# A windowed attention block feeding a gated feed-forward layer, on one core: V loaded by SyncE in fp32, masks of batch 0 added by matmul, one PSUM tile for both transposes, and a reordered opening with dummy matmuls

## The chip, the core and the metric

One core of one Trainium2 chip. The metric is device time in microseconds (us) of one execution. Before the change it was 290.46 us (median of 3 runs, 289.55 to 290.52). The profile's span, first to last instruction, is a little shorter than the timed run: 286.8 us in a run of 288.47 us. Differences are therefore taken between runs or between spans, never across.

Engine names are those of the profile: PE = TensorE, DVE = VectorE, ACT = ScalarE, POOL = GpSimd, SP = SyncE.

## The reference

```python
scores = (q @ k.T) / 8                     # q, k, v: 4 batches, 8 heads, 768 positions, 64 wide
keep   = (key < 4) | (0 <= query - key < 128)      # 4 sink keys and a window of 128
a      = softmax(where(keep, scores, -1e9))
x      = (a @ v), heads side by side       # 3072 tokens x 512
out    = (relu(x @ w_gate) * (x @ w_val)) @ w_out  # 512 -> 1536 -> 512, fp32 in and out
```

## The kernel before

Work is cut into units. A unit is a pair of heads of one batch: for batch 0 its first query half ("L", 4 units) or its second ("M", 4 units), for batches 1 to 3 all queries ("F", 12 units). Each unit's K, Q and V are loaded, cast to bf16, K and Q transposed on PE, then scores, exponentials, sums and V products follow in segments of 124 keys; the four sink keys are written into four spare rows of later segments. Beside this, PE works through the feed-forward layer in chunks: four gate matmuls, four value matmuls, then output matmuls. The four L units stand in an opening before the first chunk; all others are dealt out between chunks by a plan.

The parts that the change touches:

```python
def load_v(self, eng):                     # M and F: casting DMA from POOL straight into the bf16 tile
    dst = self.staging("v") if self.kind == "L" else self.vn
    for h in range(2):
        eng.dma_start(out=dst[:, j0:j0 + nj, h, 0:64], in_=...)

def T(self, pool, shape, tag, qcopy=nc.scalar.copy):
    ps = ptile("tk")                       # a PSUM tile for K ...
    for t in range(kn_): nc.tensor.transpose(ps[...], kn[s][...], ident[...])
    nc.scalar.copy(kT[s][...], ps[...])
    pq = ptile("tq")                       # ... and another for Q
    for t in range(qn_): nc.tensor.transpose(pq[...], qn[s][...], ident[...])
    qcopy(qT[s][...], pq[...])
    # [cut]

def S(self, gi):                           # scores of one group of segments
    # [cut: matmuls into ps, start=True, stop=True]
    nc.scalar.activation(x, ps[:, :, 0:c], Act.Exp, bias=0.0, scale=scale)
    nc.vector.tensor_tensor(x, x, bc(msk[:, m0:m0 + c], 2), op=Alu.mult)

def norm(u, part):
    ps = u.V(part)                         # sums and V products, in a two-bank attention tile
    nc.vector.transpose(r[:, 0, 0:w], ps[:, 1, 0:w])
    nc.vector.reciprocal(rc[...], r[...])
    nc.vector.transpose(r[:, 1, 0:w], ...)
    nc.vector.tensor_tensor(xTs[u.b][...], ps[:, 0, ...], r[:, 1, ...], op=Alu.mult)

# stages beside the feed-forward: after the last scores of a unit
u.S(gi)
if gi == len(u.groups) - 1:
    u.sinkv(nc.vector)                     # sink rows of V, on DVE
    if at(x + 2) is not None and x > NP:
        at(x + 2).load_v(nc.gpsimd)
```

PSUM holds three one-bank tiles for gate and value results ("gv"), one for outputs and two two-bank tiles ("at") that scores, transposes and normalisations share in turn.

The softmax here doesn't subtract the row's maximum and nothing guards it: scores larger than these inputs give would overflow.

Of the kernel before, what the change touches and what calls it, by code (L numbers as in the profile page):

```python
# [37 lines left out]
MW = 1417  # L38


@with_exitstack
def kernel(
# [33 lines left out]
    stg = [const.tile([128, 1536], F32, name=f"stg{i}") for i in range(3)]  # L76
    kn = [const.tile([128, 6, 2, 64], BF16, name=f"kn{i}") for i in range(2)]
    vn = [const.tile([128, 7, 2, 64], BF16, name=f"vn{i}") for i in range(3)]
    qn = [const.tile([128, 6, 2, 64], BF16, name=f"qn{i}") for i in range(2)]
# [11 lines left out]
    msk = const.tile([128, MW], BF16, name="msk")  # L91

# [4 lines left out]
    class Unit:  # L97


        def __init__(self, i, b, p, kind):  # L100
            self.i, self.b, self.p, self.kind, self.s, self.s3 = i, b, p, kind, i % 2, i % 3
            g = GEO[kind]
            self.q0, self.n, self.js, self.sink, self.groups, self.parts = (
                g[x] for x in ("q0", "n", "js", "sink", "groups", "parts"))
            (self.qr, self.qp, self.qn), (self.kr, self.kp, self.kn) = g["q"], g["k"]
            self.j5 = [j for j in self.js if j < 6]
            self.vn = vn[self.s3]
            self.where = {}
            for gi, segs in enumerate(self.groups):
                c = 0  # L110
                for j, qa, w in segs:
                    self.where[j] = (gi, c, qa)
                    c += w

        def staging(self, x):

            t, nk, nq = stg[self.s3], self.kn * 128, self.qn * 128
            if x == "v":
                return t[:, nk + nq:nk + nq + 128 * len(self.js)].rearrange("p (j h d) -> p j h d", h=2, d=64)
            return (t[:, 0:nk] if x == "k" else t[:, nk:nk + nq]).rearrange("p (h c) -> p h c", h=2)  # L120
# [9 lines left out]
        def load_v(self, eng):  # L130

            b, p = self.b, self.p
            dst = self.staging("v") if self.kind == "L" else self.vn
            j0, nj = self.j5[0], len(self.j5)
            for h in range(2):
                src = v[b, 2 * p + h]
                eng.dma_start(out=dst[:, j0:j0 + nj, h, 0:64],  # L137
                              in_=bass.AP(src.tensor, src.offset + 124 * j0 * D, [[D, 128], [124 * D, nj], [1, D]]))
            if 6 in self.js:
                eng.dma_start(out=dst[0:24, 6, :, 0:64],  # L140
                              in_=v[b, 2 * p:2 * p + 2, 744:768, :].rearrange("h s d -> s h d"))

        def cast(self, what, eng):

            s = self.s
            cp = eng.tensor_copy
            if what in "kq":
                dst, pp, nn = (kn[s], self.kp, self.kn) if what == "k" else (qn[s], self.qp, self.qn)
                cp(dst[0:pp, 0:nn, :, :],  # L149
                   self.staging(what)[0:pp, :, :].rearrange("p h (n d) -> p n h d", d=64))  # L150
                return
            cp(self.vn[:, 0:len(self.js), :, 0:64], self.staging("v"))
            cp(vsink[:, self.p, :, :], self.vn[0:4, 0, :, 0:64])
            self.sinkv(eng)
# [7 lines left out]
        def T(self, pool, shape, tag, qcopy=nc.scalar.copy):  # L162
# [3 lines left out]

            def ptile(name):
                t = pool.tile(shape, BF16, name=name, tag=tag)
                return t[:, 0, :] if len(shape) == 3 else t[:]
            ps = ptile("tk")  # L170
            for t in range(kn_):
                nc.tensor.transpose(ps[:, t * kp:(t + 1) * kp],  # L172
                                    kn[s][0:kp, t, :, :].rearrange("p h d -> p (h d)"), ident[0:kp, 0:kp])
# [3 lines left out]
            pq = ptile("tq")  # L177
            for t in range(qn_):
                nc.tensor.transpose(pq[:, t * qp:(t + 1) * qp],  # L179
                                    qn[s][0:qp, t, :, :].rearrange("p h d -> p (h d)"), ident[0:qp, 0:qp])  # L180
# [25 lines left out]
        def S(self, gi):  # L206
            s = self.s
            ps = ps_at.tile([128, 2, 512], F32, name="sps", tag="at")
            c = 0
            for j, qa, w in self.groups[gi]:  # L210
                for h in range(2):
                    r = slice(64 * h, 64 * h + 64)
                    nc.tensor.matmul(out=ps[:, h, c:c + w], lhsT=self.kw(j, r), rhs=qT[s][r, qa:qa + w],  # L213
                                     start=True, stop=True)
# [3 lines left out]
            m0 = MCOL[self.kind][gi]  # L218
            nc.vector.tensor_tensor(x, x, bc(msk[:, m0:m0 + c], 2), op=Alu.mult)  # L219

        def V(self, part):
# [3 lines left out]
            ps = ps_at.tile([128, 2, 512], F32, name="ops", tag="at")  # L225
            for what in range(2):
                for i, (j, qa, w) in enumerate(segs):
                    gi, c, qg = self.where[j]
                    c += qa - qg
                    for h in range(2):  # L230
                        nc.tensor.matmul(out=ps[64 * h:64 * h + 64, 1 - what, qa - q0:qa - q0 + w],  # L231
# [16 lines left out]
    def setup_pool():  # L248
        make_identity(nc, ident)
        t0, a = msk[:, 0:255], msk[:, 503:754]  # L250
        for x, w, d in ((t0, 255, 0), (a, 251, 4)):
            nc.gpsimd.memset(x, 1.0)
            nc.gpsimd.affine_select(out=x, in_=x, compare_op=Alu.is_ge, fill=0.0, base=d,
                                    pattern=[[1, w]], channel_multiplier=-1)
            nc.gpsimd.affine_select(out=x, in_=x, compare_op=Alu.is_ge, fill=0.0, base=127 - d,
# [7 lines left out]
    def setup_m0():  # L263

        ms(msk[0:4, 0:128], 1.0)
        ms(msk[0:4, 128:255], 0.0)
        cp(msk[:, 255:503], msk[:, 503:751])
        ms(msk[0:4, 255:503], 1.0)
        ms(msk[0:4, 503:627], 0.0)

    def setup_m1():

        band, sk = (lambda a, b: msk[:, 503 + a:503 + b]), (lambda n: msk[:, 255:255 + n])
        cp(msk[:, 754:1002], sk(248))
        cp(msk[:, 1002:1253], band(0, 251))
        cp(msk[:, 1253:1397], sk(144))
        cp(msk[:, 1397:1417], band(0, 20))
# [4 lines left out]
    def norm(u, part):  # L282
# [4 lines left out]
        ps = u.V(part)  # L287
        r = rpool.tile([128, 2, 416], F32, name="R")
        rc = dpool.tile([128, 13], F32, name="rc")
        nc.vector.transpose(r[:, 0, 0:w], ps[:, 1, 0:w])  # L290
# [4 lines left out]
        nc.vector.tensor_tensor(xTs[u.b][:, u.p, lo:hi], ps[:, 0, lo - c0:hi - c0], r[:, 1, lo - c0:hi - c0], op=Alu.mult)  # L295
# [36 lines left out]
    with tc.manual_schedule():  # L332
# [12 lines left out]
        for p in range(3):  # L345
            U[p].load_kq(nc.sync)
            U[p].load_v(nc.scalar if p == 0 else nc.sync)
        setup_pool()
        nc.scalar.activation(ee[0][:, 0, 0, 0:128], ident[:], Act.Exp, bias=0.0, scale=1.0)
        setup_slot(0)  # L350
        for s in range(3):
            nc.vector.memset(vn[s][:, 6, :, :], 0.0)
        nc.vector.memset(ones[:], 1.0)
# [3 lines left out]
        def next_load(x):  # L357

            w = at(x + 3)
            if w is not None:  # L360
                w.load_kq(nc.sync)
                if w.kind == "L":
                    w.load_v(nc.sync)

        casts(U[0], "kqv")
        next_load(0)
        setup_m0()
        U[0].T(*GV)
        setup_slot(1)
        casts(U[1], "kqv")  # L370
        next_load(1)
        U[1].T(*GV)
        for p in range(NP):
            for gi in range(2):
                U[p].S(gi)
            if p + 2 < NP:
                casts(U[p + 2], "kq" if p else "kqv")
                U[p + 2].T(*GV)
                if p == 0:
                    next_load(2)  # L380
            if p < 2:
                load_w(p)
            if p >= 1:
                norm(U[p - 1], 0)
                if p == 1:
                    casts(U[3], "v")
                    next_load(3)
                else:
                    U[p + 2].load_v(nc.gpsimd)
            if p >= 2:  # L390
                casts(U[p + 2], "kq")
                next_load(p + 2)
                load_w(p)
        norm(U[NP - 1], 0)
        U[6].load_v(nc.gpsimd)
        setup_m1()


        stages = []
        def unit_stages(x):  # L400
            u, prev, nxt = U[x], at(x - 1), at(x + 1)

            def s(gi):
                def f():
# [3 lines left out]
                    if gi == len(u.groups) - 1:  # L408
                        u.sinkv(nc.vector)
                        if at(x + 2) is not None and x > NP:  # L410
                            at(x + 2).load_v(nc.gpsimd)
# [6 lines left out]
            def t():  # L418
                if nxt is not None:
                    nxt.T(*AT)  # L420
                if at(x + 2) is not None:
                    casts(at(x + 2), "kq")
                    next_load(x + 2)
# [10 lines left out]
        blocks = [(0, 0, 376), (0, 376, 392)]  # L434
        for b in range(1, B):
            blocks += [(b, 0, S // 2), (b, S // 2, S // 2)]
# [4 lines left out]
        PLAN = ((0, 0), (3, 0), (12, 19), (23, 43), (47, 67), (71, 89), (72, 90))  # L441
# [6 lines left out]
        for bi, (b, c0, n) in enumerate(blocks):  # L448
            if c0 == 0 and b:
                hTs[b] = hpool.tile([128, FM, S], BF16, name="hT", tag="hT")  # L450
            for m in range(FM):
                while si < min(total, want(bi * FM + m)):
                    stages[si]()
                    si += 1
                chunk(b, c0, n, m)
                left = FM - m
                for _ in range((len(f2) + left - 1) // left):
                    f2.popleft()()
            done = c0 + n
            for t in range(6):  # L460
                lo, hi = t * 128, (t + 1) * 128
                if hi <= done and hi > c0:
# [39 lines left out]
```

## Time and profile before

The page of this kernel and a cut of its span into four stretches stand in the prediction below. PE's idle time in them (length less busy time) is 14.2 us in the opening, 7.3 and 6.4 us in the two halves of batch 0, and 3.7 us in the rest.

How the DMA engines are used is in the queue lines of the page (packets, MB, share of 16 engines over the span):

```profile
q0 software_dynamic: 30128, 7.71, 27.3%
q1 hardware_dynamic: 16224, 19.96, 21.8%
```

The software queue (POOL) moves a quarter of the bytes in two thirds of the packets and takes more of the engines' time.

### The profile page before, as it was taken

The numbers are of one execution on the slowest core, as the hardware profiler recorded it, in microseconds if no ns is written. First come the engines' busy times: TensorE is split into PE (matmuls) and PEld (weight loads), VectorE is DVE, ScalarE is ACT, GpSimd is POOL, SyncE is SP. The second block draws the span as 40 slices with busy tenths as digits, with TensorE's granted clock in tenths as the row PEclk, the third lists the DMA queues.
The fourth block names the chain that finished last, engine by engine and source line by source line (L and its number), as shares of the span: only waits on it lengthen the run. The fifth ranks groups of instructions, "written<-read, shape, count | busy, mean of one in ns | idle before, by whom it ended". The sixth has DMA issues, their size and how long they took to land.

```text
span 286.8 us, 5306 instructions
## 1 busy us (share of the span) xinstructions
PE 255.2 (89%) x2056; PEld 144.4 (50%) x2056; DVE 164.2 (57%) x347; ACT 130.3 (45%) x218; POOL 80.7 (28%) x123
## 2 busy tenths in 40 slices
PE   1567897867879989999999999999999999999994
PEld 0243454534545555555555556555555555555541
DVE  2379479966869885655666655745565642232210
ACT  3650375635655555353645545364553323333321
POOL 7959646842523532320405032300000000000000
PEclk9999999999999999999999999999999999999999
DMA  8999999993429454261914150331010000111112
GB/s 187 275 231 229 245 249 260 226 203 110 31 72 215 29 68 145 17 161 39 171 40 32 40 65 7 46 52 39 0 39 37 13 26 37 39 38 38 39 43 103
DMA packets 47178, 28.21 MB, mean 98 GB/s; under 512 B 28720, under 2 KB 44080, under 8 KB 47152
## 3 DMA queue, kind: packets, MB, share of 16 engines
q0 software_dynamic: 30128, 7.71, 27.3%
q1 hardware_dynamic: 16224, 19.96, 21.8%
q8 instruction: 16, 0.26, 0.4%
q10 hardware_dynamic: 800, 0.20, 0.3%
q14 instruction: 10, 0.08, 0.1%
HBM read 29.26 MB, written 6.29 MB: 124 GB/s over the span
## 4 chain that ended last, share of the span: by engine, by line
PE 80%; DVE 8%; ACT 4%; DMA 3%; issue 2%; POOL 1%; SPq 0%; ACTq 0%; POOLq 0%
PE gp L305 23%; PE op L324 22%; PE vp L311 21%; PE ops L231 7%; PE sps L213 4%; ACT ee L217 3%; DMA stg<-in_q_dram 3%; PE tk L172 2%; DVE R L293 2%; DVE xT L295 2%; DVE R L290 2%; PE tq L179 2%; DVE ee L219 1%; ACT kT L175 1%; DVE kTs L199 1%
## 5 line engine op out<-in xcount | busy, mean ns | idle before, releaser
L305 PE MATMUL gp<-xT,wg 128*128 128x384 bf16 (+2 forms) x384 | 80.4, 331 | 3.5 <-DVE xT L295 3.5
L308 ACT ACTIVATE gs<-gp 128x384 f32<-128x384 f32 (+2 forms) x96 | 47.3, 493 | 78.5 <-PE gp L305 77.1
L311 PE MATMUL vp<-xT,wv 128*128 128x384 bf16 (+2 forms) x384 | 79.1, 329 | 0.0
L313 DVE TENSOR_TENSOR hT<-gs,vp 128x384 bf16<-128x384 f32 (+2 forms) x96 | 52.5, 547 | 42.5 <-PE vp L311 40.0
L324 PE MATMUL op<-wo,hT 128*128 128x512 bf16 x288 | 75.9, 379 | 0.0
L217 ACT ACTIVATE ee<-sps 128x1006 bf16<-128x1006 f32 (+4 forms) x52 | 46.6, 906 | 32.0 <-PE sps L213 32.0
L219 DVE TENSOR_TENSOR ee<-ee,msk 128x1006 bf16<-128x1006 bf16 (+4 forms) x52 | 33.7, 655 | 34.1 <-ACT ee L217 34.0
L311 PEld LDWEIGHTS <-wv 128*128 128x128 bf16 x384 | 37.9, 99 | 29.2 <-issue 4.9
L137 POOL DMA_DIRECT2D vn<-in_v_dram x32 | 26.1, 818 | 80.5 <-PE ops L231 79.6
L305 PEld LDWEIGHTS <-wg 128*128 128x128 bf16 x384 | 32.8, 98 | 26.4 <-issue 5.6
L324 PEld LDWEIGHTS <-hT 128*128 128x128 bf16 x288 | 28.2, 98 | 25.1
L290 DVE STREAM_TRANSPOSE R<-ops 128x384 f32<-128x384 f32 (+1 forms) x32 | 18.7, 586 | 14.6 <-PE ops L231 14.6
L328 ACT COPY ot<-op 128x512 f32<-128x512 f32 x24 | 14.1, 586 | 22.3 <-PE op L324 22.3
L149 POOL CAST kn<-stg 128x768 bf16<-128x768 f32 (+2 forms) x20 | 15.9, 796 | 21.2 <-issue 20.9
L175 ACT COPY kT<-tk 128x768 bf16<-128x768 bf16 (+2 forms) x20 | 14.0, 700 | 16.9 <-PE tk L172 15.0
L231 PE MATMUL ops<-ee,ones 128*64 128x144 bf16 (+9 forms) x280 | 17.6, 250 | 2.6 <-ACT ee L217 1.7
L231 PEld LDWEIGHTS <-ones 128*64 128x64 bf16 x280 | 13.0, 112 | 13.7 <-issue 9.3
L213 PE MATMUL sps<-qT,kT 64*128 64x251 bf16 (+3 forms) x136 | 15.6, 257 | 4.4 <-ACT ee L217 2.6
L231 PE MATMUL ops<-ee,vn 128*64 128x144 bf16 (+9 forms) x280 | 17.2, 246 | 2.5 <-DVE vn L160 2.5
L293 DVE STREAM_TRANSPOSE R<-rc 128x384 f32<-128x384 f32 (+1 forms) x32 | 18.6, 583 | 1.1
L172 PE MATMUL tk<-ident,kn 128*128 128x128 bf16 (+2 forms) x108 | 9.7, 226 | 9.9 <-POOL kn L149 9.1
L295 DVE TENSOR_TENSOR xT<-ops,R 128x384 bf16<-128x384 f32 (+2 forms) x32 | 17.8, 558 | 1.1
(47 smaller groups left out, 151.5 us busy)
## 6 DMA issues: line engine op xcount, KB each, us to landing
out_dram<-ot SPq DMA_DIRECT2D x24, 256.0 KB, 2.0
stg<-in_k_dram SPq DMA_DIRECT2D x12, 384.0 KB, 4.6
stg<-in_q_dram SPq DMA_DIRECT2D x12, 384.0 KB, 5.3
vn<-in_v_dram POOLq DMA_DIRECT2D x24, 96.0 KB, 3.6
wg<-in_moe_w_gate_dram POOLq DMA_DIRECT2D x4, 384.0 KB, 7.8
wv<-in_moe_w_val_dram POOLq DMA_DIRECT2D x4, 384.0 KB, 8.9
wo<-in_moe_w_out_dram POOLq DMA_DIRECT2D x3, 512.0 KB, 7.7
stg<-in_k_dram SPq DMA_DIRECT2D x4, 280.0 KB, 5.2
```

Source lines behind the costliest of these rows:

```text
L137: eng.dma_start(out=dst[:, j0:j0 + nj, h, 0:64], in_=bass.AP(src.tensor, src.offset + 124 * j0 * D, [[D, 128], [124 * D, nj], [1, D]]))
L213: nc.tensor.matmul(out=ps[:, h, c:c + w], lhsT=self.kw(j, r), rhs=qT[s][r, qa:qa + w], start=True, stop=True)
L217: nc.scalar.activation(x, ps[:, :, 0:c], Act.Exp, bias=0.0, scale=scale)
L219: nc.vector.tensor_tensor(x, x, bc(msk[:, m0:m0 + c], 2), op=Alu.mult)
L231: nc.tensor.matmul(out=ps[64 * h:64 * h + 64, 1 - what, qa - q0:qa - q0 + w], lhsT=self.vn[:, j, h, :] if what else ones[:], rhs=ee[s][:, ...
L290: nc.vector.transpose(r[:, 0, 0:w], ps[:, 1, 0:w])
L293: nc.vector.transpose(r[:, 1, 0:w], bass.AP(a.tensor, a.offset, [a.ap[0], [1, nb], [0, 32]]))
L305: nc.tensor.matmul(out=gp[:, 0:n], lhsT=wg[:, ko, m * 128:(m + 1) * 128], rhs=x[:, ko, c0:c0 + n], start=ko == 0, stop=ko == KO - 1)
L308: nc.scalar.activation(gs[:, 0:n], gp[:, 0:n], Act.Relu, bias=0.0, scale=1.0)
L311: nc.tensor.matmul(out=vp[:, 0:n], lhsT=wv[:, ko, m * 128:(m + 1) * 128], rhs=x[:, ko, c0:c0 + n], start=ko == 0, stop=ko == KO - 1)
L313: nc.vector.tensor_tensor(hT[:, m, c0:c0 + n], gs[:, 0:n], vp[:, 0:n], op=Alu.mult)
L324: nc.tensor.matmul(out=op, lhsT=hTs[b][:, m, t * 128:(t + 1) * 128], rhs=wo[:, m, :], start=m == 0, stop=m == FM - 1)
```

## The change

Its intent: take work off DVE and waits off PE in the opening and beside batch 0, and get the transfers in earlier. Cut to its core:

```diff
-    stg = [const.tile([128, 1536], F32, name=f"stg{i}") for i in range(3)]
+    stg = [const.tile([128, 2432], F32, name=f"stg{i}") for i in range(4)]
     # kn, qn: 2 -> 3 buffers, vn: 3 -> 4
 def load_v:
-            dst = self.staging("v") if self.kind == "L" else self.vn
+            dst, o = self.staging("v"), self.js[0]          # fp32, by SP, all units
 def cast("v"):                                              # on POOL
+            cp(self.vn[:, j0:j0 + nj, :, :], self.staging("v")[:, 0:nj, :, :])
+            if 6 in self.js:
+                cp(self.vn[0:24, 6, :, :], self.staging("v")[0:24, nj, :, :])
             self.sinkv(eng)                                 # now for every kind, on POOL
 def T:
-            ps = ptile("tk")    # ... copy ...    pq = ptile("tq")
+            both = pool.tile(shape, BF16, name="tkq", tag=tag)    # all transposes, then both copies
 def S:
+            if biased:                                      # kinds L and M
+                for h in range(2):
+                    nc.tensor.matmul(out=ps[:, h, 0:n], lhsT=ident[:], rhs=bias[:, m0:m0 + n], start=True, stop=False,
+                                     skip_group_check=True)
-                                     start=True, stop=True)
+                                     start=not biased, stop=True, skip_group_check=True)
-            nc.vector.tensor_tensor(x, x, bc(msk[:, m0:m0 + c], 2), op=Alu.mult)
+            if not biased:
+                nc.vector.tensor_tensor(x, x, bc(msk[:, m0:m0 + c], 2), op=Alu.mult)
 def V (in the opening):
+                ps = [pool.tile([128, 512], F32, name=x, tag="gv")[:] for x in ("sums", "ops")][::-1]
 opening:
+        warm(16) ... warm(6) ... 4 x warm(8) ... warm(16)   # dummy matmuls of 128 columns
         # K and Q casts of units 2 and 3 come before V casts, loads of units 0 to 3 first of all
 stages:
+                if x >= 5:
+                    held(x + 8 - 5)                         # load K, Q, V of the unit three ahead
+                if at(x + 3) is not None:
+                    casts(at(x + 3), "kqv")
-        PLAN = ((0, 0), (3, 0), (12, 19), (23, 43), ...
+        PLAN = ((0, 0), (2, 0), (10, 19), (23, 43), ...
# [cut: the bias tile with 0 and -1e30, the mask made from it, order of loads]
```

## The prediction

> **What bounds the kernel now.** I read the page first (busy shares, the 40 slices), then one table of stretches, then the TensorE and VectorE timelines of the first 30 us, then TensorE's waits. The page:
>
> ```profile
> PE 255.2 (89%) x2056; PEld 144.4 (50%) x2056; DVE 164.2 (57%) x347; ACT 130.3 (45%) x218; POOL 80.7 (28%) x123
> PE   1567897867879989999999999999999999999994
> DMA  8999999993429454261914150331010000111112
> ```
>
> A slice is 7.2 us. From the fifteenth on PE is full; before it, it is not. So I cut the span where the work changes: start of the first gate/value matmuls, start of batch 0's second half, start of batch 1. Columns: length, busy time of each engine, clock, DMA share.
>
> ```profile
> 0.00:27.50 27.50, 13.27 (x104) 7.67 (x105) 15.24 (x44) 11.27 (x22) 22.28 (x47) 1.00 1.15 232
> 27.50:62.30 34.80, 27.55 (x268) 16.95 (x268) 26.28 (x55) 18.72 (x31) 22.33 (x32) 1.00 1.33 244
> 62.30:104.60 42.30, 35.87 (x370) 21.41 (x370) 32.72 (x67) 23.18 (x34) 16.08 (x21) 1.00 0.51 84
> 104.60:286.80 182.20, 178.55 (x1318) 98.41 (x1316) 89.99 (x183) 77.11 (x132) 20.00 (x26) 1.00 0.24 54
> ```
>
> The last 182 us are TensorE-bound (3.65 us idle, nearly all after the last matmul). No chunk of that part changes, so whatever the change is worth must come from the first 104.6 us: 14.2 us of idle PE in the opening, 7.3 + 6.4 us in batch 0. In the opening the chain of waits runs through VectorE, which normalises four head pairs and multiplies masks:
>
> ```profile
> 20.82 0.55 DVE xT L295
> 21.37 2.14 DVE ee L219 x2
> 23.51 0.50 DVE R L290
> ...
> 26.86 0.56 DVE xT L295
> 27.46 0.47 PE gp L305
> ```
>
> Look at the 2.14 us of masks in the middle. Then TensorE itself is slow when it starts:
>
> ```profile
> 27.73 1.46 PE L311 MATMUL vp<-xT,wv 128*128 128x376 bf16 x4
> 28.98 1.46 PE L305 MATMUL gp<-xT,wg 128*128 128x376 bf16 x4
> 30.24 1.16 PE L311 MATMUL vp<-xT,wv 128*128 128x376 bf16 x4
> 31.23 0.80 PE L305 MATMUL gp<-xT,wg 128*128 128x376 bf16 x4
> ```
>
> Starts are 1.25, 1.26, 0.99 us apart, and from 31.23 on 0.64 us, though the granted-clock column says 1.00 throughout. TensorE's waits between 28 and 105 us:
>
> ```profile
> PE ops L231 <- DVE vn L160: 2.5, 2, 1.2
> PE tq L179 <- ACT kT L175: 2.3, 3, 0.9
> PE ops L231 <- ACT ee L217: 1.7, 2, 1.1
> PE gp L305 <- DVE xT L295: 1.7, 1, 1.7
> PE sps L213 <- DVE kTs L199: 1.3, 2, 1.0
> PE tq L179 <- ACT ee L217: 0.7, 1, 0.7
> ```
>
> None names a DMA, although the DMA engines are full for 65 us.
>
> **What the Trainium skill says.** "TensorE: Matmul & The Clock Gate", section Part 1: an idle array runs at 1.2 GHz and goes to 2.4 GHz after about 3.4 us of sustained activity. The trace agrees: 376 columns took 313 ns (1.25/4), then 160. The same page, Part 3: matmuls in different row groups run concurrently. Here the two heads' 64-row score matmuls do (at 120.90 a 251-column pair, and the next pair starts 0.12 us later); a bias matmul uses all 128 rows and cannot. "DMA: Bandwidth & Descriptors", section SWDGE vs HWDGE vs iDMA: a cast inside a DMA is possible only from GpSimd, and there software writes the descriptors. Before does that for V: each pair of V issues holds Pool about 1.6 us. "SBUF — State Buffer", section Who interferes with whom: a VectorE instruction with two SBUF inputs and a GpSimd instruction that reads SBUF exclude each other. The trace fits: the two mask multiplies at 21.29 lasted 2.22 us beside casts, against means of 745 + 469 ns, and the query cast there 1.09 against a 0.74 mean.
>
> **The change part by part.** The fp32 loads and the block-transpose normalisation exist already; new are these.
>
> (a) Masks of batch 0 become bias matmuls. VectorE loses four multiplies of about 0.75 + 0.47 us before the first chunk (4.7 us with the contention) and eight of about 0.6 us in the second stretch. TensorE gains, per second-half unit, 2 x (399 + 415) columns: 1628 / 2.4 GHz = 0.68 us, x 4 = 2.7 us, on the bound engine. The first-half ones fall into idle time.
>
> (b) The opening is reordered: K/Q casts of units 2 and 3 come ahead on Pool, normalisation uses other PSUM banks, 70 dummy matmuls keep PE busy. I walked the engines with durations of the trace. Pool: setup to 3.9 (as now); unit 0 to 6.5, unit 1 to 8.9, K/Q of unit 2 to 9.95, first weight issues to 11.6, K/Q of unit 3 to 12.8 (now 14.1). PE: transposes of unit 1 to 8.0; at the cold rate its list is then solid (scores 1.6 with bias, 8 dummies 0.85, transposes 0.85, normalisation sums 1.25 each), so it should turn warm at about 12.5. From there ScalarE leads: transposed copies 1.2 us and exponentials 1.01 + 0.39 per unit: unit 3's copies end at 15.3, unit 2's exponentials at 16.7, unit 3's at 18.5. Sums of unit 3: 18.5 to 19.2. VectorE needs 2.05 us per normalisation (0.58 + 0.23 + 0.58 + 0.55, and gaps): 14.1 to 16.1, 16.1 to 18.2, 18.2 to 20.2, 20.2 to 22.25. First chunk's fourth matmul at 22.3 instead of 27.46: -5.2 us.
>
> (c) Warm start: the three slow groups above lose 0.61 + 0.62 + 0.35: -1.6 us.
>
> (d) Waits in batch 0. K and Q transposes share one PSUM tile, so the Q transposes no longer wait for a copy: 2.3 + 0.7 = -3.0 us. The sink rows of V are written on Pool a unit or more ahead: -2.5 us. Attention stages start a chunk earlier and the last pair's normalisation is issued two chunks before the second half needs it, not right at it: -1.7 us. Without masks sums wait only for the exponentials: -0.4 us.
>
> (e) New waits: scores waiting for a PSUM pair still held by a normalisation, and sums issued directly after exponentials, about 0.4 us two or three times: +1 us.
>
> (f) V by SP in fp32. V is 23,296 rows of 128 B (4 second-half units x 2 heads x 536 rows, 12 later units x 2 x 792) out of the software queue's 30,128, which take 27.3% of the DMA engines (1253 us of engine time, 42 ns each). ScalarE's queue moved 800 mostly 256 B packets of V in 0.3%, 17 ns each. Half a unit's data therefore gets cheaper, not dearer, and Pool swaps 2.2 us of issue for about 1.4 us of cast. This is a supply for the earlier schedule, not a gain.
>
> Sum: -5.2 - 1.6 + 2.7 - 7.6 + 1.0 = -10.7 us. From 290.46: 279.8, I say 280.
>
> **The rivals.**
> 1. TensorE stays cold in the opening. For it: in before it was about half busy from 18 to 24 us and was still slow at 28. Against: the dummies and bias matmuls leave it hardly a gap after 8 us. Then PE's own list sets the pace: sums of unit 3 end at 24.5, VectorE is done at 26.6; four of the 5.2 us go, and perhaps (c): about 285.
> 2. Supply takes the place of VectorE's wait. First weights are issued at 10 and 11 us; at 7.8 to 8.9 us to landing they arrive at 18 to 20, just before they are needed at 22, and now beside fuller loads on SP. SP also waits for earlier loads before it issues more. Against: before's engines were fullest with the dear small packets, and later weight slices leave at about 19 and 23 us, no later than now (23.3 and 28.1). It would cost 2 to 4 us: 282 to 284.
> 3. Bias matmuls cost more than they free. For it: TensorE is the bound and VectorE only 75% busy in the second stretch. Against: 2.7 us against waits of 7.6. If half of these reappear under other names, 284.
> 4. The later units stall, because V casts in Pool and three-unit lookahead replace five-unit K/Q lookahead. Against: Pool is busy 20 of the last 182 us, and a unit lasts about 16 us there. Small.
>
> **Range and chances.** Rivals 1 and 2 are not exclusive, and each takes 2 to 5 us; on the other side ScalarE-bound walking may be pessimistic and most idle PE of batch 0 could go (another 3 to 4 us). Range 275.5 to 286. Faster by 2% means below 284.65: only rival 1 with another, or half of the waits back, breaks it. Chances: faster 0.83, within 2% 0.15, slower 0.02.
>
> **What would show it.** First gate matmul group complete at about 22 to 23 us, its four starts 0.16 us apart from the beginning (right) or 0.31 (rival 1). No PE wait on a DMA or on Pool after 15 us (rival 2 if there is). Second half of batch 0 (392 columns) starting at about 53 us, not 62; batch 1 (384 columns) at about 94, not 104.6; from there to the end 182 us as before. PE waits on the sink copy and Q transposes gone, sum of PE waits in batch 0 about 6 us. Software-queue share of DMA down from 27.3% to under 12%. Wrong would be: the gain in the last 182 us, or batch 0 as long as now after an earlier start.

## The result, and the profile after

276.10 us, median of 4 runs (275.65 to 277.17), against 290.06 us for the kernel before (4 runs). The ratio is 0.9525, with a 95% interval of 0.949 to 0.9559. Ratios here and below are the mean time of one kernel's fast runs over that of the other's of the same rounds, so not quite the ratio of the medians.

The page of the changed kernel, the same three lines as before (a slice is now 6.8 us):

```profile
PE 259.8 (95%) x2158; PEld 148.4 (54%) x2158; DVE 148.2 (54%) x329; ACT 129.6 (47%) x218; POOL 67.8 (25%) x123
PE   5997899899989999999999999999999999999994
DMA  8999999998465170531707125101101110011122
```

PE is nearly full from the second slice. The stretches, cut near the same events (first value matmuls, first 392-column chunk, first 384-column chunk); columns are length, busy time of PE, weight loads, DVE, ACT, POOL, granted clock (the TensorE clock that the profile shows as allowed, 1.00 being full), DMA share, GB/s:

```profile
0.00:22.90 22.90, 17.84 (x190) 11.62 (x191) 12.97 (x38) 10.70 (x22) 19.18 (x45) 1.00 1.10 223
22.90:54.80 31.90, 29.15 (x303) 18.18 (x301) 18.18 (x47) 19.55 (x33) 16.53 (x29) 1.00 1.15 242
54.80:91.50 36.70, 34.27 (x357) 20.19 (x352) 30.01 (x66) 22.12 (x33) 15.53 (x25) 1.00 0.68 168
91.50:273.90 182.40, 178.56 (x1318) 98.42 (x1316) 87.02 (x181) 77.18 (x132) 16.56 (x26) 1.00 0.22 67
```

The last stretch is 182.4 us against 182.2: nothing was won there. The cuts are not quite the same events: 62.3 in the kernel before is the fourth gate matmul of the first 392-column chunk (the first three start at 59.97), 54.8 in the changed one is the first of the four. Cut at the first value matmul of that chunk in both (62.48 and 55.50 us), at the first value matmul of all (27.73 and 22.93) and at the first gate matmul of batch 1 (104.58 and 91.47), the opening is 4.8 us shorter, the first half of batch 0 2.2, the second half 6.1. PE's idle time beside batch 0 went from 13.7 to 5.2 us (31.90 - 29.15 and 36.70 - 34.27). The start of the first chunk on PE's timeline:

```profile
22.77 0.32 PE L323 MATMUL gp<-xT,wg 128*128 128x376 bf16 x1 [1.38 <-DVE xT L313]
22.93 0.80 PE L329 MATMUL vp<-xT,wv 128*128 128x376 bf16 x4
23.57 0.80 PE L323 MATMUL gp<-xT,wg 128*128 128x376 bf16 x4
```

The fourth gate matmul still waits for the last normalisation, but starts at 22.77 us and not 27.46, and the groups behind it are 0.64 us apart from the beginning. PE's waits from 22 to 95 us:

```profile
PE gp L323 <- DVE xT L313: 1.4, 1, 1.4
PE ops L248 <- DVE xT L313: 1.3, 2, 0.7
PE tkq L180 <- DVE xT L313: 1.1, 2, 0.6
PE sps L221 <- DVE xT L313: 1.1, 3, 0.4
PE ops L248 <- ACT ee L230: 0.9, 2, 0.6
PE sps L226 <- ACT qT L188: 0.8, 1, 0.8
```

The waits for sink copies (`vn`) and for a second transpose tile (`tq`) are gone. What is left is mostly work waiting for an attention tile that a normalisation still holds (released by `xT`): 3.5 us. And the queues:

```profile
q1 hardware_dynamic: 40224, 25.93, 34.2%
q0 software_dynamic: 5808, 4.72, 11.0%
```

Some 24,000 packets, nearly all of them rows of V, went from one queue to the other. The software queue lost 0.273 x 286.8 x 16 - 0.110 x 273.9 x 16 = 771 us of engine time, 32 ns a packet; the hardware queue gained 0.342 x 273.9 x 16 - 0.218 x 286.8 x 16 = 498 us, 21 ns a packet, for twice the bytes written. These are differences of whole queues, so a change in their other packets is in them too; numbers 7 and 8 below, which differ in V's path alone, give 771 and 491 us.

### The profile page after: what moved, and what is told of

Same layout as the page of the kernel before. It is cut to its first block, busy times and chain, and to the rows that moved or that the text cites. A ratio compares the mean times of both kernels' runs of the same rounds, so it can differ in the third digit from the quotient of the medians.

```text
span 273.9 us, 5552 instructions
## 1 busy us (share of the span) xinstructions
PE 259.8 (95%) x2158; PEld 148.4 (54%) x2158; DVE 148.2 (54%) x329; ACT 129.6 (47%) x218; POOL 67.8 (25%) x123
## 4 chain that ended last, share of the span: by engine, by line
PE 84%; DVE 8%; ACT 3%; issue 1%; DMA 1%; POOL 1%; SPq 0%; DVEq 0%; ACTq 0%
PE gp L323 22%; PE op L342 22%; PE vp L329 21%; PE ops L248 7%; PE sps L226 5%; PE sps L221 2%; DVE R L311 2%; PE tkq L180 2%; DVE R L308 2%; PE tkq L183 2%; DVE xT L313 2%; ACT ee L230 2%; DMA stg<-in_q_dram 1%; DVE ee L232 1%; DVE rc L309 1%
## 5 line engine op out<-in xcount | busy, mean ns | idle before, releaser
L323 PE MATMUL gp<-xT,wg 128*128 128x384 bf16 (+2 forms) x384 | 78.8, 327 | 1.4 <-DVE xT L313 1.4
L329 PE MATMUL vp<-xT,wv 128*128 128x384 bf16 (+2 forms) x384 | 78.1, 326 | 0.0
L232 DVE TENSOR_TENSOR ee<-ee,msk 128x1006 bf16<-128x1006 bf16 (+2 forms) x36 | 26.0, 723 | 26.0 <-ACT ee L230 25.8
L308 DVE STREAM_TRANSPOSE R<-ops 128x384 f32<-128x384 f32 (+1 forms) x28 | 16.4, 584 | 14.3 <-PE ops L248 14.3
L186 ACT COPY kT<-tkq 128x768 bf16<-128x768 bf16 (+2 forms) x20 | 14.0, 700 | 18.1 <-PE tkq L183 17.9
L157 POOL CAST vn<-stg 128x768 bf16<-128x768 f32 (+2 forms) x20 | 14.4, 720 | 22.7 <-DMA stg<-in_v_dram 16.7
L248 PEld LDWEIGHTS <-ones 128*64 128x64 bf16 x280 | 12.1, 109 | 12.3 <-issue 7.4
L226 PEld LDWEIGHTS <-kT 64*128 64x128 bf16 x136 | 6.6, 93 | 19.2 <-issue 16.8
L248 PE MATMUL ops<-ee,ones 128*64 128x251 bf16 (+9 forms) x256 | 14.3, 238 | 2.2 <-DVE xT L313 1.3
L153 POOL CAST qn<-stg 128x768 bf16<-128x768 f32 (+2 forms) x20 | 14.5, 724 | 5.2 <-DMA stg<-in_q_dram 4.8
## 6 DMA issues: line engine op xcount, KB each, us to landing
wv<-in_moe_w_val_dram POOLq DMA_DIRECT2D x4, 384.0 KB, 11.8
```

Source lines behind the costliest of these rows:

```text
L153: cp(dst[0:pp, 0:nn, :, :], self.staging(what)[0:pp, :, :].rearrange("p h (n d) -> p n h d", d=64))
L226: nc.tensor.matmul(out=ps[:, h, c:c + w], lhsT=self.kw(j, r), rhs=qT[s][r, qa:qa + w], start=not biased, stop=True, skip_group_check=True)
L248: nc.tensor.matmul(out=ps[1 - what][64 * h:64 * h + 64, qa - q0:qa - q0 + w], lhsT=self.vn[:, j, h, :] if what else ones[:], rhs=ee[s][:, ...
L323: nc.tensor.matmul(out=gp[:, 0:n], lhsT=wg[:, ko, m * 128:(m + 1) * 128], rhs=x[:, ko, c0:c0 + n], start=ko == 0, stop=ko == KO - 1)
L329: nc.tensor.matmul(out=vp[:, 0:n], lhsT=wv[:, ko, m * 128:(m + 1) * 128], rhs=x[:, ko, c0:c0 + n], start=ko == 0, stop=ko == KO - 1)
```

## The experiments

Twelve kernels, each the changed kernel with one thing undone unless said otherwise. All gave correct results. To read them, it helps to cut each profiled run in two: the start of the fourth gate matmul of the first chunk ("opening"), and from there to the first gate matmul of batch 1 ("batch 0"). Of the kernel before these are 27.46 and 77.12 us, of the changed one 22.77 and 68.70.

| kernel | median us | ratio to before (95%) | less the changed one, us | opening us | batch 0 us |
|---|---|---|---|---|---|
| changed | 276.10 | 0.9525 (0.949 to 0.9559) | 0 | 22.77 | 68.70 |
| 1 no dummies | 276.34 | 0.9544 (0.9503 to 0.9585) | +0.24 | 22.27 | 69.63 |
| 2 no dummies, masks multiplied | 280.31 | 0.9665 (0.964 to 0.9689) | +4.21 | 25.34 | 71.37 |
| 3 masks multiplied | 279.02 | 0.9631 (0.9593 to 0.9669) | +2.92 | 24.92 | 69.09 |
| 4 bias in the first half only | 276.14 | 0.954 (0.9504 to 0.9576) | +0.04 | 23.48 | 68.35 |
| 5 opening normalises in "at" tiles | 280.41 | 0.9667 (0.9631 to 0.9702) | +4.31 | 26.11 | 69.31 |
| 6 two transpose tiles | 279.50 | 0.9639 (0.9611 to 0.9666) | +3.40 | 23.36 | 71.63 |
| 7 late sinks | 280.16 | 0.9663 (0.9631 to 0.9694) | +4.06 | 22.73 | 72.48 |
| 8 late sinks, V by POOL | 279.06 | 0.963 (0.9597 to 0.9663) | +2.96 | 24.74 | 72.23 |
| 9 old plan | 279.13 | 0.9624 (0.9585 to 0.9662) | +3.03 | 23.90 | 71.36 |
| 10 fewer dummies | 275.80 | 0.952 (0.9487 to 0.9552) | -0.30 | 21.71 | 69.18 |
| 11 fewer dummies, bias in the first half only | 275.55 | 0.9515 (0.9481 to 0.955) | -0.55 | 22.05 | 69.70 |
| before with dummies | 288.71 | 0.9967 (0.9934 to 1.0) | +12.61 | 29.31 | 75.39 |

The kernel before had medians of 289.86 to 290.39 us. The two last columns are of one profiled run each; that of number 8 (280.93 us) was the slowest of its six. One run of number 4 (280.56 us) was over 1.5% above its fastest and is left out of the ratio.

A caution for the opening column. Numbers 4, 6, 7 and 9 give TensorE the same work as the changed kernel up to the fourth gate matmul, yet theirs starts at 23.48, 23.36, 22.73 and 23.90 us. The array came to full rate at different times: after the eight dummies that start at 10.43 to 10.48 us the next group follows in 0.47 us in number 7, 0.56 in the changed kernel, but 0.85 or 0.86 in numbers 4, 6 and 9, which were still at half rate. So differences up to about 1.2 us between single profiles show nothing in this column.

### What brings the array to full rate: numbers 1, 2, 3 and the kernel before with dummies

```diff
-            for _ in range(n):
+            for _ in range(0):          # number 1: no dummy is issued
```

> The changed kernel (276.1 us) without any of its 70 dummy matmuls. Theory (the prediction's step b and c): the dummies bring TensorE to full rate before the first chunk; without them it stays at half rate, the first chunk's fourth gate matmul comes at 25 us or later instead of 22.77 and its 376-column matmuls start 0.31 us apart: 279 to 282 us. Rival: the bias matmuls and the tighter order keep TensorE busy enough by themselves; then the list only gets shorter and the first chunk comes about 1 us earlier: 274.5 to 276.

The rival held: 276.34 us, indistinguishable from the changed kernel, first chunk 0.5 us earlier (within the spread just named) and its groups 0.64 us apart. So the dummies are not what warms the array in the changed kernel, against the prediction's step (b). The opposite edit keeps the dummies and takes the bias matmuls out:

```diff
-BIASED = "LM"
+BIASED = ""
+        # setup_m0: msk[:, 0:754] made from bias, so that L units have their mask
```

> The changed kernel with all masks of batch 0 multiplied on VectorE again (no bias matmuls). Theory (step a): VectorE gets four masks of about 1.2 us back into the opening, where its normalisations end the wait, so the first chunk comes 2 to 4 us later; in the second stretch 2.7 us of TensorE are saved but waits for masks come back: 278 to 281 us. Rival (number 3 of the prediction): bias costs as much as it frees, 275 to 277.

279.02 us: the theory. The opening is 2.15 us longer (1.0 us, if the changed kernel's is taken at the late end of the spread) and its chain now runs from DVE's masks to DVE's normalisations; batch 0 is only 0.4 us longer. But the dummies did not keep the array at full rate (lines between left out):

```profile
20.68 0.47 PE L248 MATMUL sums<-ee,ones 128*64 128x255 bf16 x6 [1.80 <-DVE ee L232]
23.73 1.51 PE L324 MATMUL gp<-xT,wg 128*128 128x376 bf16 x4
25.08 0.80 PE L330 MATMUL vp<-xT,wv 128*128 128x376 bf16 x4
```

After the wait of 1.80 us for a mask the granted clock was 0.50 from about 21.3 to 24.7 us. The first gate group fell into that; the value matmuls behind it ran at full rate. This profiled run had a mean granted clock of 0.994; in the other three timed runs it was 0.986 to 0.988, by estimate (missing share of the clock x span x 2) some 7 to 8 us at half rate instead of 3.3. So this kernel loses the bias matmuls and, in part, the full rate. The fourth corner has neither:

> The changed kernel with neither dummies nor bias matmuls, the fourth corner beside no dummies (276.3) and all multiply (279.0). If either of the two fills TensorE enough to get full rate: here it is at half rate at the first chunk, starts 0.31 us apart, 1.5 us or more above all multiply: 280 to 282. If neither matters and the order alone keeps it busy: 278 to 279.5 with 0.16 us.

280.31 us, and PE's timeline at the first chunk shows half rate (two lines left out):

```profile
25.34 0.47 PE L324 MATMUL gp<-xT,wg 128*128 128x376 bf16 x1 [0.92 <-DVE xT L314]
25.61 1.46 PE L330 MATMUL vp<-xT,wv 128*128 128x376 bf16 x4
26.86 1.46 PE L324 MATMUL gp<-xT,wg 128*128 128x376 bf16 x4
29.35 0.80 PE L324 MATMUL gp<-xT,wg 128*128 128x376 bf16 x4
```

Starts are 1.25 us apart, as in the kernel before, and 0.64 us only after 29.35. With bias matmuls the first chunk is at full rate with or without dummies. With dummies alone it was so from its value matmuls on, in the run profiled. With neither, batch 0 costs 2.7 us more than in the changed kernel and 2.3 more than in number 3. The timed runs of numbers 2 and 3 do not separate them (0.964 to 0.9689 and 0.9593 to 0.9669). Earlier in this run the array had already been at full rate (six sums of 0.74 us until 15 us, of 0.47 at 17.75) and then lost it:

```profile
17.75 0.47 PE L248 MATMUL sums<-ee,ones 128*64 128x255 bf16 x6 [1.45 <-DVE ee L232]
20.57 1.04 PE L248 MATMUL sums<-ee,ones 128*64 128x255 bf16 x6 [1.66 <-DVE ee L232]
```

Both waits are for masks on DVE. The granted clock fell to 0.50 at about 19.1 us, after the first wait and some 0.2 us into the second, and came back at about 29.3. So in the profiles of numbers 2 and 3 masks by multiply cost the opening twice: their own time, and the clock. The times do not show the second part: of number 2's four runs two had a mean granted clock of 0.981 and 0.982, two of 0.997 and 0.998, and all lie between 279.95 and 280.79 us. Finally the dummies alone in the kernel before:

> The kernel before with the dummy matmuls alone, at the same places of its opening. Theory (step c): they bring TensorE to full rate before the first value matmuls, whose starts then come 0.16 us apart instead of 0.31: 1.2 to 1.8 us less than before, 288 to 288.8 us. Rival, after the run without dummies: what warmed TensorE in the changed kernel was its denser work, and 70 short dummies beside 2.6 us waits for Pool change nothing: 289.5 to 290.5, starts 0.31 us apart.

288.71 us, ratio 0.9967, with an interval that reaches 1.0. The time and the starts are those of the theory, but the difference is not clear of noise. In the profiled run the first chunk's groups are 0.64 us apart, so the dummies did warm it; but the opening is 1.85 us longer, because groups of 8 dummies stand at half rate, about 0.9 us each, ahead of sums that DVE waits for. The gain in batch 0 (1.73 us) is eaten there in that run, and the timed gain of about 1 us is barely clear of nothing.

### Bias matmuls in the second half: number 4

```diff
-BIASED = "LM"
+BIASED = "L"
```

> The changed kernel with bias matmuls only for the first query half (the opening, where TensorE idles) and mask multiplies for the second half. If the 2.7 us of bias matmuls in the second half only cost: about 274 us. If the waits for the masks outweigh them, as the prediction held: 276.5 to 278. Start of the first chunk unchanged at 22.8 us in both.

Between the two: 276.14 us. The bias matmuls are saved (2.7 us by the prediction's estimate), and PE's waits between 25 and 58 us rise from 2.8 to 5.0 us (scores behind a held tile, sums behind a mask). For the second query half the bias is a wash, and the third rival of the prediction is right for that part. Its worth lies in the opening, where PE has time and DVE has none.

### Where the opening normalises: number 5

```diff
-                norm(U[p - 1], 0, ps_gv)
+                norm(U[p - 1], 0)           # also for the last pair: two-bank attention tile
```

> The changed kernel with the normalisations of the opening in the two-bank attention tiles again instead of in the gate/value tiles. Theory (step b): scores of the next pair then wait for a tile that a normalisation still holds, as in before (1.1 us waits of the scores, twice): first chunk at 24 us or later, 277.3 to 279. Rival: VectorE sets the end of the opening anyway, 276 to 276.8.

More than the theory said: 280.41 us, opening 26.11 us, 3.3 us longer (2.2, if the changed kernel's is taken at the late end of the spread). PE's timeline shows the two waits of the kernel before again:

```profile
16.66 0.28 PE L221 MATMUL sps<-bias,ident 128*128 128x132 bf16 x2 [1.16 <-ACT ee L230]
20.35 0.28 PE L221 MATMUL sps<-bias,ident 128*128 128x132 bf16 x2 [1.17 <-ACT ee L230]
```

The second group of scores waits until the exponentials of the first give up their tile, since the other tile is with a normalisation. This is the largest of the parts of the opening that were undone, and the prediction named it in half a clause ("normalisation uses other PSUM banks").

### The waits beside batch 0: numbers 6, 7, 8 and 9

Number 6 gives K and Q transposes separate tiles again, in the stages only.

```diff
-            both = pool.tile(shape, BF16, name="tkq", tag=tag)
+            ps = pool.tile(shape, BF16, name="tk", tag=tag)[:, 0, :]
+            # K transposes, K copy, then: pq = pool.tile(... "tq" ...), Q transposes, Q copy
```

> The changed kernel with K and Q transposes in two PSUM tiles again, in the stretch beside the feed-forward only (the opening as changed). Theory (step d, first term): the Q transposes wait again for a tile, up to 3.0 us in batch 0, waits of TensorE at the Q transposes come back: 278 to 279.5 us. Rival: with the masks off VectorE and the sinks early, tiles come free in time and the wait was only one face of the queue: 276 to 277.

279.50 us, the theory and slightly above: Q transposes wait at six of nine units for 0.35 to 0.89 us, 3.5 us in sum.

Number 7 writes sink rows on DVE after a unit's last scores.

```diff
                     u.S(gi)
+                    if gi == len(u.groups) - 1:
+                        u.sinkv(nc.vector)
# and the cast of V calls sinkv for L units only
```

> The changed kernel with the sink rows of V of the second half and of batches 1 to 3 written on VectorE after the last scores of a unit, as before the change; V still comes by SP. Theory (step d, second term): the wait of the V sums for this copy returns, about 1.25 us each time it is hit: 277.5 to 279 us. Rival: the hits came from a full VectorE and are gone with it: 276 to 276.5.

280.16 us, a good microsecond above the range. The wait is hit four times (0.58, 1.12, 1.24, 1.24 us), where the kernel before had shown two. DVE's and PE's timelines at the last of them:

```profile
88.84 0.59 DVE L232 TENSOR_TENSOR ee<-ee,msk 128x830 bf16<-128x830 bf16 x1 [0.46 <-ACT ee L230]
89.35 0.27 DVE L168 COPY vn<-vn 4x384 bf16<-4x384 bf16 x1
89.67 0.36 PE L248 MATMUL ops<-ee,vn 128*64 128x248 bf16 x6 [1.24 <-DVE vn L168]
```

The copy takes 0.27 us and needs nothing of this unit's scores. But it stands in DVE's list behind the mask of the last group, which waits for ScalarE's exponentials; the V products of the first part, which do not need that group at all, wait with it. A full DVE is not needed for it: a place behind a waiting instruction is enough.

Number 8 is number 7 with V of M and F units by casting DMAs from POOL.

```diff
+            if self.kind != "L":
+                self.load_v(nc.gpsimd)      # in place of the cast, straight into the bf16 tile
+                return
```

> As the run with late sinks, and V of these units by casting DMAs from Pool straight into its tile (the way before the change), issued three units ahead. Theory (step f): supply, not a gain: within 0.7 us of the run with late sinks, though the software queue's share of the DMA engines goes back to about 27%. Rival (number 2 turned round): the dear small packets delay weights or K and Q of the second half, TensorE waits on Pool or DMA appear between 23 and 55 us, 2 us or more slower than the run with late sinks.

279.06 us against 280.16, intervals overlapping (0.9597 to 0.9663 and 0.9631 to 0.9694); the software queue's share is back at 27.9%, and PE waits for no DMA between 21 and 97 us. If anything V by POOL is 1 us faster here, not slower. So the fp32 path is not a gain by itself, as step (f) had it. What it makes possible is the cast and the sink rows early, on POOL, in list order: sinks on POOL straight behind a casting DMA would have had to wait there for its data. No run tried that.

Number 9 puts the old plan of stages back.

```diff
-        PLAN = ((0, 0), (2, 0), (10, 19), (23, 43), ...
+        PLAN = ((0, 0), (3, 0), (12, 19), (23, 43), ...
```

> The changed kernel with the earlier plan of stages (attention beside the feed-forward from chunk 3, second half's pairs done at chunk 12). Theory (step d, third term): the second half of batch 0 waits again for its last normalisation at its start, 1.3 to 2 us on the fourth gate matmul of the first 392-column chunk: 277.5 to 278.5 us. Rival: the plan only moves work; the fewer stages in the first half are made up: 276 to 276.6.

279.13 us. From PE's waits of 50 to 97 us:

```profile
PE gp L323 <- DVE xT L313: 2.3, 1, 2.3
PE op L342 <- DMA wo<-in_moe_w_out_dram: 1.3, 1, 1.3
```

The first is the expected one, at the first 392-column chunk. The second was in nobody's list: in the changed kernel the output weights are issued by the stages, behind the casts, so a later plan delivers them too late. Of the profiled run's loss 1.1 us lie in the opening, which this edit leaves alone (the late full rate above), and 2.7 us in batch 0.

### Candidates: numbers 10 and 11

Number 10 drops the four inner groups of 8 dummies; number 11 also has bias matmuls in the first half only.

> The changed kernel without the four groups of 8 dummies between the pairs (the first 16 and 6 and the last 16 stay). In its chain TensorE sets the pace from 7 to 18 us and these groups are 2.1 us of it. If TensorE stays at full rate without them: first chunk 0.8 to 1.5 us earlier, 274.5 to 275.5 us. If they are needed for the rate: the first chunk at 24 us or later, 277 to 280.

> A candidate to beat both: bias matmuls only for the first half, and without the four inner groups of dummies. The runs of the two edits alone were 0.0 and 0.3 us from the changed kernel. Both theories: first chunk at 21.7 to 22.5 us; if what is saved on TensorE is not given back: 274 to 275; if it is given back in waits for masks and tiles, 275.5 to 276.3.

275.80 and 275.55 us. The openings are 1.1 and 0.7 us shorter, batch 0 0.5 and 1.0 us longer. Both are nominally below 276.10, but the intervals lie over one another: no version was shown to beat the changed kernel. Why an earlier start is partly given back in batch 0 (number 1 too, +0.9 us, most of it one 0.74 us wait of scores for a tile) is not settled; these are single profiled runs.

## Why the prediction was right

The direction, the place and the size held: 280 us predicted, 276.10 measured, inside 275.5 to 286. By its steps, in us:

| step | predicted | measured |
|---|---|---|
| opening, fourth gate matmul | -5.2 | -4.7 (27.46 to 22.77); -3.6 with the latest of the same openings, 23.90 |
| (c) warm start of the first groups | -1.6 | -1.6 (starts 0.64 apart) |
| (a) bias matmuls of the second query half | +2.7 | not measured singly (their 16 matmuls are 4.1 us of PE's modelled busy time); returned in waits (number 4: 0.0) |
| (d) and (e) waits beside batch 0 | -6.6 | -8.4 (waits of 28 to 105 us in before, 13.6, against 5.2 behind the first gate group) |
| first gate matmul of batch 1 | -10.7 | -13.1 (104.58 to 91.47) |
| last 182 us | 0 | +0.2 |

- **The opening** came out nearly as walked. Its cause did not. The prediction gave the warm array to dummies plus bias matmuls; number 1 shows the dummies superfluous beside the bias matmuls, number 3 that dummies alone do not hold the full rate. It also put the weight on the masks (its 4.7 us of them in the opening are 5.2 in the trace); number 3 gives these 2.15 us, number 5 gives the choice of PSUM tiles 3.3 us. The two overlap. That the size came out so near is in part luck.
- **Not undone**: the order of casts and loads in the opening. In the kernel before the last unit's transposes waited 2.60 us for their K cast, which stood behind two weight issues on POOL, and started at 13.73 us; in number 2, which has the new order and neither filling, they start at 12.01. What that is worth in the time, no run tells.
- **Rival 1**, a cold opening, did not happen, but number 2 shows that it was near: without both fillings it is there, and with dummies alone the array fell back as well.
- **Rival 2**, supply: PE waited for no DMA, though weight slices now took 9.7 us (gate) and 11.8 us (value) to land against 7.8 and 8.9. Number 9 shows how close it is.
- **Rival 3** is right for the second half of batch 0 and wrong for the opening.
- **Mis-sized**: the term (d) less (e). Undone one at a time, tiles cost 3.4 us (3.0 predicted), sinks 4.1 (2.5), the plan 3.0 (1.7); in batch 0 alone, by the single profiles, 2.9, 3.8 and 2.7. I had read each from the waits that the kernel before happened to show, and a wait hidden behind another is not in such a list. The forecast of times shows where: second half of batch 0 predicted from 53 to 94 us, 41 us long; it ran from 54.83 to 91.47, 36.6 us.
- **Not additive**: the five costly undoings (numbers 3, 5, 6, 7, 9) sum to 17.7 us, more than the 14.0 us that the change won. Each brings back a wait that others had partly covered.
- **Open**: of the 2.4 us between -10.7 and -13.1, waits give 1.8 less 0.5 for the opening; the rest, about 1 us, is PE's modelled busy time beside batch 0 (63.2 us before, 63.4 after, where -1.6 + 2.7 should have added 1.1; both from the first value matmul on). Fewer restarts after waits would do that; no run tells.

## What to carry to other kernels

In a kernel whose late part is bound by PE, look for the waits in the part before it, and undo each fix alone to learn its size: the list of waits of the old kernel understates them. Ask of each small copy what it stands behind in its engine's list, and of each PSUM tile who holds it while the next work wants it; both were worth more here than the mask that took DVE's time. Fill an idle PE with useful work rather than dummies, and check whether that work alone keeps the array at its rate.

## What the Trainium skill lacked or had wrong

- "TensorE: Matmul & The Clock Gate", Part 1: its table of states puts the return to half rate after an idle window of about 3.4 us; a later passage speaks of short idle times that also bring it, without their lengths. Here a window did not have to be idle for that: in number 3 the granted clock fell at about 21.3 us, and in the 3.4 us before that PE was busy for 1.2 us and its longest gap was 1.80 us; in number 2 it fell at about 19.1 us, after 3.4 us with 1.6 us busy and a longest gap of 1.45 us. The half-rate stretches then lasted 3.4 and 10.2 us, one and three times the page's window. The kernel before stayed at half rate from 13.7 to 24.3 us while the profile had PE busy for 7.7 of 10.6 us. The page gives no share of busy time that decides.
- The same page calls the window free-running and lets the point of transition vary by 500 ns either way (elsewhere it tells of 6, 11 or 14 slow matmuls in runs of one kernel). With the same TensorE work in the opening the spread was wider here: eight dummies that start at 10.45 us were already coming to full rate in number 7 (next group 0.47 us later), while in number 9 full rate came only after 13 us; the first chunk's fourth gate matmul followed at 22.73 and 23.90 us. That the window's phase is the reason fits, but is not shown.
- No page says how a profile's granted clock shows this. Here it read 1.00 all through the first half-rate phase (matmuls of 376 columns 313 ns apart in the kernel before), and 0.50 for the later fall-back (19.1 to 29.3 us of number 2, 21.3 to 24.7 us of number 3).
- "DMA: Bandwidth & Descriptors" gives no cost per small row by kind of queue. The same rows of 64 elements took about 32 ns of engine time each by the software queue with a cast to bf16, and 21 ns by the hardware queue in fp32 (differences of whole queues).
